# K_p transposed by DMA, batch 0's attention over both halves, and a divided last store in a fused Linformer attention and maxout kernel

## Chip, cores and metric

One core of a Trainium2 chip. The metric is the device time of one execution in microseconds; several executions are made and the median is given. Every kernel gave a correct result. Spans of profiles are some 1.8 us shorter than the device time of the same execution.

## The reference

```python
def _attn_ref(q, k, v, E, F):             # q, k, v: 8 x 8 x 1024 x 64
    k_proj = einsum('ks,bhsd->bhkd', E, k)      # K_p: 64 rows for 1024 tokens
    v_proj = einsum('ks,bhsd->bhkd', F, v)      # V_p
    attn = softmax(scale * q @ k_proj^T)
    return attn @ v_proj                        # x: 8192 x 512 after a transpose

def _moe_ref(x, w1, w2, w_out):           # 512 -> 1024 -> 512
    g = maximum(x @ w1, x @ w2)
    return g @ w_out                            # 8192 x 512, fp32
```

## The kernel before

Batches follow one another. While TensorE computes the output layer ("down") of one batch's units and the first layer ("up") of the next unit, the attention of the next batch is worked in between. The program is emitted slot by slot: a slot is one down product (12 matmuls, 1.31 us) and two up products (0.44 us each); 14 slots and one attention make a batch. "Slot -8" of a batch below means eight slots before its first one. The kernel uses max(a, b) = max(a - b, 0) + b: the up product is x(w1 - w2) (`wd`), and b's part goes through the product M = w2 w_out. From batch 1 on, the products are done with seven block products in place of eight.

These are the parts that the change and the argument touch. The copies out of the projection, and the transpose of K_p on TensorE through a PSUM bank:

```python
def step_kv(t, h0=0, h1=H, which="kv", att=False):
    kv_ps = att_banks()[:, 0, :] if att else mm_bank()
    ...                                              # the projection, 16 matmuls
    if "k" in which:
        eng(out=fl(t["kp"]), in_=kv_ps[0:KP, 0:n])               # ScalarE
    elif "v" in which: ...                                       # cut
        nc.vector.tensor_copy(out=fl(t["vp"][KP:128]), in_=kv_ps[KP:128, 0:n])
        nc.vector.tensor_copy(out=fl(t["vp"][0:KP]), in_=kv_ps[KP:128, 0:n])

def step_kpt(t, h0=0, h1=H, att=False):
    kpt_ps = att_banks(FP16)[:, 0, :] if att else mm_bank(FP16)
    for h in range(h0, h1):
        for r in range(2):
            nc.tensor.transpose(out=kpt_ps[...], in_=t["kp"][:, h, :], identity=ident16[:KP, :KP])
    nc.vector.tensor_copy(out=t["kpt"][...], in_=kpt_ps[...])
```

The loads of q, k and v, 2 MB each in DRAM and cast to fp16 on the way, are issued from GpSimd. Stores and the DMA transposes of q are issued from SyncE (SP in the profile), one after the other. The schedule for batches 3 to 7:

```python
at(b - 1, -11, 0, step_qt_dma, t, 0, H // 2)
at(b - 1, -11, 0, step_qt_dma, t, H // 2, H)
at(b - 1, -9, 0, step_kv, t, 0, H, "kv", True)
at(b - 1, -9, 0, loads, b + 1, "v", "q", "k")     # the next batch's v and q, and the k after it
at(b - 1, -8, 0, step_kpt, t, 0, H, True)
plan = "sc0 -7, da0 -6, sc1 -4, da1 -3, sc2 -1, da2 0, sc3 2, da3 3"   # sc0: the first scores; da0: their sums and the product with V_p
```

The softmax here doesn't subtract the row's maximum and nothing guards it: scores larger than these inputs give would overflow.

Of the kernel before, what the change touches and what calls it, by code (L numbers as in the profile page):

```python
# [16 lines left out]
def kernel(  # L17
# [82 lines left out]

    def load(t, n, src, b, h0, h1, c0=0, c1=NC):
        nc.gpsimd.dma_start(  # L102
            out=t[n][:, h0:h1, c0:c1, :],
            in_=src[b, h0:h1].rearrange("h (p c) d -> p h c d", c=NC)[:, :, c0:c1, :],
        )
# [4 lines left out]
    for h0 in (0, H // 2):  # L110
        load(tiles[0], "k", k, 0, h0, h0 + H // 2)
        load(tiles[0], "q", q, 0, h0, h0 + H // 2, 0, NC // 2)
        if h0 == 0:
            ident = const.tile([128, 128], FP32)
            make_identity(nc, ident)
# [6 lines left out]
    for f0 in range(0, DF, 256):  # L122
        if f0 == 256:
            load(tiles[0], "q", q, 0, 0, H, NC // 2, NC)
        for w_sb, w in ((w2_sb, moe_w2), (w1_sb, moe_w1)):
            nc.gpsimd.dma_start(
                out=w_sb[:, :, f0 : f0 + 256],
                in_=w[:, f0 : f0 + 256].rearrange("(r p) f -> p r f", p=128),
            )
# [34 lines left out]
    def new_attn(t):  # L164
        t["kp"] = proj.tile([KP, H, D], FP16, tag="kp", name="kp_sb")
        t["vp"] = proj.tile([128, H, D], FP16, tag="vp", name="vp_sb")
        t["kpt"] = proj.tile([128, H, KP], FP16, tag="kpt", name="kpt_sb")
        t["qt"] = qtp.tile([128, H, HALF], FP16, tag="qt", name="qt_sb")
        t["ex"] = {}


    def step_kv(t, h0=0, h1=H, which="kv", att=False):
# [14 lines left out]
        if "k" in which:  # L187
            eng = nc.vector.tensor_copy if which == "k" else nc.scalar.copy
            eng(out=fl(t["kp"]), in_=kv_ps[0:KP, 0:n])
        if both:  # L190
            nc.vector.tensor_copy(out=fl(t["vp"]), in_=kv_ps[:, 0:n])
        elif "v" in which:
            nc.vector.tensor_copy(out=fl(t["vp"][KP:128]), in_=kv_ps[KP:128, 0:n])
            nc.vector.tensor_copy(out=fl(t["vp"][0:KP]), in_=kv_ps[KP:128, 0:n])


    def step_kpt(t, h0=0, h1=H, att=False):
        kpt_ps = att_banks(FP16)[:, 0, :] if att else mm_bank(FP16)
        for h in range(h0, h1):
            for r in range(2):  # L200
                nc.tensor.transpose(
                    out=kpt_ps[r * D : (r + 1) * D, (h - h0) * KP : (h - h0 + 1) * KP],
                    in_=t["kp"][:, h, :],
                    identity=ident16[:KP, :KP],
                )
        nc.vector.tensor_copy(
            out=t["kpt"][:, h0:h1, :].rearrange("q h k -> q (h k)"),
            in_=kpt_ps[:, 0 : (h1 - h0) * KP],
        )

# [77 lines left out]
    def two_sc(t, g, j):  # L288
        sc_ps = att_banks()
        t["ps", g] = sc_ps  # L290
        for h in range(2):
            for o in range(2):
                for e in range(2):
# [7 lines left out]
                    )  # L301
        ex = stage.tile([128, 2, HALF], FP16, tag="ex", name="ex_sb")
        t["ex"][g] = ex
        nc.scalar.activation(out=ex, in_=sc_ps, func=ACTF.Exp, scale=scale)


    def two_dn(t, g):
        dn_ps = t.pop(("ps", g))
        for r in range(2):
            for e in range(2):  # L310
# [3 lines left out]
                    lhsT=ones16[rows, 0:D],  # L314
                    rhs=t["ex"][g][rows, e, :],
                    start=True, stop=True,
                )
        ld = soft.tile([128, 2, HALF], FP32, tag="ld", name="ld_sb")
        nc.scalar.activation(out=ld, in_=dn_ps, func=ACTF.Ln)
        nc.scalar.activation(out=ld, in_=ld, func=ACTF.Exp, scale=-1.0)  # L320
        rec = ld
        t["rec", g] = rec

    def two_at(t, g, j):
        ex, rec = t["ex"].pop(g), t.pop(("rec", g))
        at_ps = [mm_bank().rearrange("q (h n) -> q h n", h=2) for _ in range(2)]
# [26 lines left out]
    def up_slots(t, j):  # L353
        t["gt", j] = gt = gpool.tile([128, NFB, HALF], FP16, tag="gt", name="gt_sb")
        for fb in range(NFB):
            def up(fb=fb):
                h_ps = mm_bank()
                for r in range(NDC):
# [5 lines left out]
                    )  # L364
                nc.vector.tensor_scalar_max(gt[:, fb, :], h_ps, 0.0)
            yield up
# [237 lines left out]
    def down_steps(u, alone):  # L604
# [6 lines left out]

        def product(k, name, n):
            if n is not None:
# [13 lines left out]
            }[k]()  # L627
            for i in range(2):
                for c in range(NG + NX):
# [3 lines left out]
                        rhs=w_(c),  # L633
                        start=(n is not None and i == 0 and c == 0),
                        stop=(c == NG + NX - 1), skip_group_check=True,
# [12 lines left out]

        def store(j):
            nc.sync.dma_start(  # L650
                out=out.rearrange("(n p i o) m -> n o p i m", p=128, i=NI, o=2)[
                    b, o, :, 2 * j : 2 * j + 2, :
                ],
                in_=st["o", j],
            )
# [18 lines left out]
        def p3():  # L674
            add(0, 1, product(3, "Z", None), st["u1"])
            store(0)
            o_tile(1)
            add(1, 1, st["u2"], st["s5"])

        def p4():  # L680
            bank = product(4, "X", None)
            nc.scalar.copy(out=cols(st["o", 1], 0), in_=two(bank))
            store(1)
# [8 lines left out]
    warm(2)  # L692
    step_kpt(t, 0, 4)
    step_qt(t, 0, 4, 0, NI // 2)
    warm(2)
    two_sc(t, 0, 0)
    warm(2)
    step_kv(t, 4, 8, "k")
    two_dn(t, 0)
    step_qt(t, 4, 4, 0, NI // 2)  # L700
    step_kpt(t, 4, 8)
    warm(3)
    two_sc(t, 1, 0)
    warm(3)
    step_kv(t, 0, 4, "v")
    two_dn(t, 1)
    two_at(t, 0, 0)
    warm(3)
    step_kv(t, 4, 8, "v")
    step_w2t(0)  # L710
    step_wd(0)
    two_at(t, 1, 0)
    warm(6)

# [7 lines left out]
    def loads(b, *names):  # L722
# [5 lines left out]
    slots = [  # L728
        (0, u0[0]), (1, u0[1]), (None, f(step_qt, 0, 4, NI // 2, NI)),
        (None, f(step_qt, 4, 4, NI // 2, NI)), (None, lambda: loads(1, "v", "q", "k")),  # L730
        (None, lambda: warm(2)),
        (None, f(two_sc, 0, 1)), (None, f(two_sc, 1, 1)), (None, wd[1]), (2, u0[2]),
        (None, f(two_dn, 0)), (3, u0[3]), (None, f(two_dn, 1)), (None, wd[2]),
        (None, f(two_at, 0, 1)), (4, u0[4]), (5, u0[5]), (None, wt[1]), (None, wd[3]),
        (None, f(two_at, 1, 1)), (None, wt[2]), (6, u0[6]), (None, wt[3]), (7, u0[7]),
        *((8 + n, x) for n, x in enumerate(u1)),
        *((16 + n, lambda n=n: step_m(n)) for n in range(NDC)),
# [25 lines left out]
    for b in range(1, B):  # L763
# [26 lines left out]
        else:  # L790
            at(b - 1, -11, 0, new_attn, t)
            at(b - 1, -11, 0, step_qt_dma, t, 0, H // 2)
            at(b - 1, -11, 0, step_qt_dma, t, H // 2, H)
            at(b - 1, -9, 0, step_kv, t, 0, H, "kv", True)
            at(b - 1, -9, 0, loads, b + 1, "v", "q", "k")
            at(b - 1, -8, 0, step_kpt, t, 0, H, True)
            plan = "sc0 -7, da0 -6, sc1 -4, da1 -3, sc2 -1, da2 0, sc3 2, da3 3"
        for x in plan.split(", "):
            name, n = x.split()
# [64 lines left out]
```

## Time and profile before

| | before |
|---|---|
| device time, median | 347.74 us |
| span of the profile | 345.4 us |
| mean granted TensorE clock | 0.996 |
| TensorE (PE) busy | 332.9 us, 96% |
| period of one batch | 37.9 us |
| first matmul of the product M | 44.16 us |
| last matmul ends / last store lands | 340.45 / 344.10 us |

The page gives for each engine the time in which it was busy, and the chain of work that ended last, followed back from the end: whatever has a large share of that chain sets the time. Here TensorE has it, with no large wait. In the lines PE is TensorE, PEld its weight loads, DVE VectorE, ACT ScalarE, POOL GpSimd and SP SyncE, with a q behind the name for what stands in an engine's queue; L12 is line 12 of the kernel. The lines themselves stand in the prediction.

### The profile page before, as it was taken

The numbers are of one execution on the slowest core, as the hardware profiler recorded it, in microseconds if no ns is written. First come the engines' busy times: TensorE is split into PE (matmuls) and PEld (weight loads), VectorE is DVE, ScalarE is ACT, GpSimd is POOL, SyncE is SP. The second block draws the span as 40 slices with busy tenths as digits, with TensorE's granted clock in tenths as the row PEclk, the third lists the DMA queues.
The fourth block names the chain that finished last, engine by engine and source line by source line (L and its number), as shares of the span: only waits on it lengthen the run. The fifth ranks groups of instructions, "written<-read, shape, count | busy, mean of one in ns | idle before, by whom it ended". The sixth has DMA issues, their size and how long they took to land.

```text
span 345.4 us, 7094 instructions
## 1 busy us (share of the span) xinstructions
PE 332.9 (96%) x2979; PEld 233.5 (68%) x2979; DVE 232.4 (67%) x394; ACT 218.7 (63%) x325; POOL 31.5 (9%) x43
## 2 busy tenths in 40 slices
PE   8988999999999999999999999999999999999994
PEld 4543444434476777777777777777777777888883
DVE  1367717534787778686769778686869777777561
ACT  2437222773896778668884777668875788654541
POOL 8433002011103000120012000100000000000000
PEclk9999999999999999999999999999999999999998
DMA  8999999999998999799669949891923030303033
GB/s 154 200 197 201 207 207 193 238 159 260 174 205 183 195 208 250 109 191 193 173 114 181 222 122 172 150 200 20 199 47 123 2 121 2 121 5 123 0 123 121
DMA packets 65232, 52.36 MB, mean 152 GB/s; under 512 B 26160, under 2 KB 56880, under 8 KB 65200
## 3 DMA queue, kind: packets, MB, share of 16 engines
q0 software_dynamic: 31312, 28.31, 53.7%
q1 hardware_dynamic: 33888, 23.60, 25.2%
q8 instruction: 23, 0.38, 0.4%
q14 instruction: 9, 0.07, 0.1%
HBM read 57.15 MB, written 16.78 MB: 214 GB/s over the span
## 4 chain that ended last, share of the span: by engine, by line
PE 75%; DVE 9%; ACT 6%; DMA 6%; POOL 2%; issue 1%; DVEq 0%; ACTq 0%; POOLq 0%
PE mm_ps L630 31%; PE mm_ps L552 21%; PE mm_ps L385 5%; DMA big<-in_moe_w_dram 4%; PE mm_ps L359 4%; PE att_ps L265 4%; PE att_ps L180 3%; DVE big L496 2%; PE att_ps L241 2%; DVE xt_sb L279 2%; ACT ld_sb L272 2%; DVE gt_sb L567 2%; PE mm_ps L425 2%; ACT ld_sb L275 2%; PE mm_ps L520 2%
## 5 line engine op out<-in xcount | busy, mean ns | idle before, releaser
L506 ACT COPY p_sb<-mm_ps 128x512 f32<-128x512 f32 x160 | 89.1, 592 | 44.0 <-PE mm_ps L630 29.6
L630 PEld LDWEIGHTS <-big 128*128 128x128 f16 x672 | 65.7, 98 | 8.1 <-DVE big L496 0.5
L630 PE MATMUL mm_ps<-T_sb,big 128*128 128x256 f16 x504 | 61.6, 273 | 0.3 <-DVE big L496 0.3
L279 DVE TENSOR_TENSOR xt_sb<-att_ps,ld_sb 128x1024 f16<-128x1024 f32 x28 | 34.2, 1221 | 29.2 <-ACT ld_sb L275 29.1
L567 DVE TENSOR_TENSOR gt_sb<-mm_ps,p_sb 128x512 f16<-128x512 f32 x52 | 35.8, 689 | 22.4 <-PE mm_ps L552 22.4
L552 PEld LDWEIGHTS <-big 128*128 128x128 f16 x416 | 38.9, 98 | 12.7 <-issue 8.5
L552 PE MATMUL mm_ps<-big 128*128 128x256 f16 x312 | 43.7, 273 | 0.3 <-DVE gt_sb L567 0.3
L552 PEld LDWEIGHTS <-wd_sb 128*128 128x128 f16 x312 | 28.2, 98 | 13.8 <-issue 10.7
L630 PEld LDWEIGHTS <-gt_sb 128*128 128x128 f16 x336 | 32.7, 98 | 4.2 <-DVE gt_sb L570 0.2
L630 PE MATMUL mm_ps<-wo_sb,gt_sb 128*128 128x256 f16 x224 | 33.7, 273 | 0.0
L552 PE MATMUL mm_ps<-xt_sb,wd_sb 128*128 128x256 f16 x208 | 31.0, 273 | 2.3 <-DVE gt_sb L567 2.3
L249 ACT ACTIVATE ex_sb<-att_ps 128x1024 f16<-128x1024 f32 x28 | 28.9, 1031 | 4.2 <-PE att_ps L241 4.2
L272 ACT ACTIVATE ld_sb<-att_ps 128x1024 f32<-128x1024 f32 x28 | 28.9, 1030 | 3.5 <-PE att_ps L265 3.5
L275 ACT ACTIVATE ld_sb<-ld_sb 128x1024 f32<-128x1024 f32 x28 | 30.0, 1070 | 0.4
L646 DVE TENSOR_TENSOR o_sb<-mm_ps,p_sb 128x512 f32<-128x512 f32 x28 | 19.3, 689 | 12.1 <-PE mm_ps L630 12.1
L630 PE MATMUL mm_ps<-m_sb,xt_sb 128*128 128x256 f16 x112 | 21.4, 273 | 0.0
L102 POOL DMA_DIRECT2D v_sb<-in_v_dram x9 | 7.7, 863 | 145.1 <-DMA qt_sb<-q_sb 120.8
L570 DVE TENSOR_SCALAR gt_sb<-gt_sb 128x512 f16<-128x512 f16 (+1 forms) x52 | 19.1, 367 | 1.8
L496 DVE TENSOR_TENSOR big<-gt_sb 128x1024 f16<-128x1024 f16 x28 | 19.2, 685 | 0.9
L602 ACT ACTIVATE gt_sb<-mm_ps 128x512 f16<-128x512 f32 x26 | 15.6, 599 | 4.7 <-PE mm_ps L552 4.7
L630 PEld LDWEIGHTS <-xt_sb 128*128 128x128 f16 x168 | 16.4, 98 | 1.9
L567 DVE TENSOR_TENSOR gt_sb<-p_sb 128x512 f16<-128x512 f32 x26 | 17.7, 681 | 0.0
(94 smaller groups left out, 455.4 us busy)
## 6 DMA issues: line engine op xcount, KB each, us to landing
out_dram<-o_sb SPq DMA_DIRECT2D x28, 512.0 KB, 3.1
k_sb<-in_k_dram POOLq DMA_DIRECT2D x7, 1024.0 KB, 18.2
v_sb<-in_v_dram POOLq DMA_DIRECT2D x7, 1024.0 KB, 9.9
q_sb<-in_q_dram POOLq DMA_DIRECT2D x7, 1024.0 KB, 13.6
big<-in_moe_w_dram POOLq DMA_DIRECT2D x8, 256.0 KB, 14.3
out_dram<-o_sb SPq DMA_DIRECT2D x8, 256.0 KB, 4.6
k_sb<-in_k_dram POOLq DMA_DIRECT2D x2, 512.0 KB, 7.8
v_sb<-in_v_dram POOLq DMA_DIRECT2D x2, 512.0 KB, 12.5
```

The lines of the kernel that those rows point to most:

```text
L249: nc.scalar.activation(out=ex, in_=sc_ps, func=ACTF.Exp, scale=scale)
L272: nc.scalar.activation(out=ld, in_=dn_ps, func=ACTF.Ln)
L275: nc.scalar.activation(out=ld, in_=ld, func=ACTF.Exp, scale=-1.0)
L279: nc.vector.tensor_tensor(out=t["xt"][:, p, :, :], in0=at_ps, in1=ld, op=ALU.mult)
L385: nc.tensor.matmul(out=op_ps, lhsT=lhsT, rhs=rhs, start=(n == 0), stop=(n == NFB + NDC - 1),)
L496: nc.vector.tensor_tensor(out=S(i), in0=x, in1=y, op=op)
L506: nc.scalar.copy(out=x, in_=bank)
L552: nc.tensor.matmul(out=bank[:, m * W : (m + 1) * W], lhsT=w_[:, n_, (2 * d + m) * 128 : (2 * d + m + 1) * 128], rhs=a[:, n_, :], start=(n ...
L567: nc.vector.tensor_tensor(out=c_blk(j, c), in0=two(x), in1=two(y), op=ALU.add)
L570: nc.vector.tensor_scalar_max(ap, ap, 0.0)
L630: nc.tensor.matmul(out=bank[:, i * CH : (i + 1) * CH], lhsT=a(c)[:, i * 128 : (i + 1) * 128], rhs=w_(c), start=(n is not None and i == 0 a ...
L646: nc.vector.tensor_tensor(out=cols(st["o", j], c), in0=two(x), in1=two(y), op=ALU.add)
```

## The change

It has three independent parts. At the start, batch 0's q is loaded whole ahead of the weights, its attention runs over both halves of the blocks, and the up slots alternate between the halves. In the middle, K_p of batches 3 to 7 is transposed by a DMA and not by TensorE; for this the K_p tile holds each head twice, and the copies of V_p are deferred by one slot (this in batches 1 and 2 as well). At the end, the last output tile is stored in three parts.

```diff
-        load(tiles[0], "q", q, 0, h0, h0 + H // 2, 0, NC // 2)
+        load(tiles[0], "q", q, 0, h0, h0 + H // 2)
...
-        t["kp"] = proj.tile([KP, H, D], FP16, tag="kp", name="kp_sb")
+        t["kp"] = proj.tile([KP, H, 2, D], FP16, tag="kp", name="kp_sb")
...
         elif "v" in which:
-            nc.vector.tensor_copy(out=fl(t["vp"][KP:128]), in_=kv_ps[KP:128, 0:n])
-            nc.vector.tensor_copy(out=fl(t["vp"][0:KP]), in_=kv_ps[KP:128, 0:n])
+            def finish_v():
+                nc.vector.tensor_copy(out=fl(t["vp"][KP:128]), in_=kv_ps[KP:128, 0:n])
+                if att:
+                    nc.vector.tensor_copy(out=kp[:, :, 1, :], in_=kp[:, :, 0, :])
+                    step_kpt_dma(t)
+                nc.vector.tensor_copy(out=fl(t["vp"][0:KP]), in_=fl(t["vp"][KP:128]))
+
+            return finish_v
...
+    def step_kpt_dma(t):
+        nc.sync.dma_start_transpose(
+            out=t["kpt"], in_=t["kp"].rearrange("p h r d -> p (h r d)")
+        )
...                                  # start: attention over both halves, alternating up slots
+                if fb < 3:
+                    nc.scalar.activation(out=gt[:, fb, :], in_=h_ps, func=ACTF.Relu)
+                else:
+                    nc.vector.tensor_scalar_max(gt[:, fb, :], h_ps, 0.0)
...                                  # end: the last tile in three stores
+            if alone:
+                store(1, m0=CH)
...
-            at(b - 1, -11, 0, new_attn, t)
-            at(b - 1, -11, 0, step_qt_dma, t, 0, H // 2)
-            at(b - 1, -11, 0, step_qt_dma, t, H // 2, H)
-            at(b - 1, -9, 0, step_kv, t, 0, H, "kv", True)
-            at(b - 1, -9, 0, loads, b + 1, "v", "q", "k")
-            at(b - 1, -8, 0, step_kpt, t, 0, H, True)
+            at(b - 1, -12, 0, new_attn, t)
+            at(b - 1, -12, 0, step_qt_dma, t, 0, H // 2)
+            at(b - 1, -12, 0, step_qt_dma, t, H // 2, H)
+            at(b - 1, -9 if b == 3 else -10, 2 if b == 3 else 0, step_kv, t, 0, H, "kv", True)
+            at(b - 1, -7, 0, loads, b + 1, "v", "q", "k")
             plan = "sc0 -7, da0 -6, sc1 -4, da1 -3, sc2 -1, da2 0, sc3 2, da3 3"
+            if b == 3:
+                plan = "sc0 -5, da0 -4, sc1 -3, da1 -2, sc2 -1, da2 0, sc3 2, da3 3"
```

More of the change, by code (lines that the diff above doesn't have):

```diff
@@ L99, in load_all, with load @@
         load(t, n, src, b, 0, H)
-    def load(t, n, src, b, h0, h1, c0=0, c1=NC):
+    def load(t, n, src, b, h0, h1):
         nc.gpsimd.dma_start(
-            out=t[n][:, h0:h1, c0:c1, :],
-            in_=src[b, h0:h1].rearrange("h (p c) d -> p h c d", c=NC)[:, :, c0:c1, :],
+            out=t[n][:, h0:h1],
+            in_=src[b, h0:h1].rearrange("h (p c) d -> p h c d", c=NC),
         )
@@ L122 @@
     for f0 in range(0, DF, 256):
-        if f0 == 256:
-            load(tiles[0], "q", q, 0, 0, H, NC // 2, NC)
         for w_sb, w in ((w2_sb, moe_w2), (w1_sb, moe_w1)):
@@ L188, in step_kv @@
             eng = nc.vector.tensor_copy if which == "k" else nc.scalar.copy
-            eng(out=fl(t["kp"]), in_=kv_ps[0:KP, 0:n])
+            kp = t["kp"][:, h0:h1]
+            eng(out=kp[:, :, 0, :], in_=kv_ps[0:KP, 0:n].rearrange("p (h d) -> p h d", d=D))
         if both:
@@ L192, in step_kv, with step_kpt @@
         elif "v" in which:
-            nc.vector.tensor_copy(out=fl(t["vp"][KP:128]), in_=kv_ps[KP:128, 0:n])
-            nc.vector.tensor_copy(out=fl(t["vp"][0:KP]), in_=kv_ps[KP:128, 0:n])
-    def step_kpt(t, h0=0, h1=H, att=False):
-        kpt_ps = att_banks(FP16)[:, 0, :] if att else mm_bank(FP16)
+            def finish_v():
[5 more added lines that the diff above has]
+            return finish_v
+    def step_kpt(t, h0=0, h1=H):
+        kpt_ps = mm_bank(FP16)
         for h in range(h0, h1):
@@ L202, in step_kpt @@
                     out=kpt_ps[r * D : (r + 1) * D, (h - h0) * KP : (h - h0 + 1) * KP],
-                    in_=t["kp"][:, h, :],
+                    in_=t["kp"][:, h, 0, :],
                     identity=ident16[:KP, :KP],
@@ L289, in two_sc @@
         sc_ps = att_banks()
-        t["ps", g] = sc_ps
+        t["ps", g, j] = sc_ps
         for h in range(2):
@@ L301, in two_sc, with two_dn @@
                     )
-        ex = stage.tile([128, 2, HALF], FP16, tag="ex", name="ex_sb")
-        t["ex"][g] = ex
-        nc.scalar.activation(out=ex, in_=sc_ps, func=ACTF.Exp, scale=scale)
-    def two_dn(t, g):
-        dn_ps = t.pop(("ps", g))
+        pool, tag = (ppool, "pu") if (g, j) == (1, 1) else (stage, "ex")
+        t["ex", g, j] = pool.tile([128, 2, HALF], FP16, tag=tag, name="ex_sb")
+        nc.scalar.activation(out=t["ex", g, j], in_=sc_ps, func=ACTF.Exp, scale=scale)
+    def two_dn(t, g, j):
+        dn_ps = t.pop(("ps", g, j))
         for r in range(2):
@@ L314, in two_dn, with two_inv @@
                     lhsT=ones16[rows, 0:D],
-                    rhs=t["ex"][g][rows, e, :],
+                    rhs=t["ex", g, j][rows, e, :],
                     start=True, stop=True,
                 )
-        ld = soft.tile([128, 2, HALF], FP32, tag="ld", name="ld_sb")
-        nc.scalar.activation(out=ld, in_=dn_ps, func=ACTF.Ln)
-        nc.scalar.activation(out=ld, in_=ld, func=ACTF.Exp, scale=-1.0)
-        rec = ld
-        t["rec", g] = rec
+        pool, tag = (soft, "ld") if g == 0 else (opool, "o")
+        t["rec", g, j] = pool.tile([128, 2, HALF], FP32, tag=tag, name="ld_sb")
+        nc.scalar.activation(out=t["rec", g, j], in_=dn_ps, func=ACTF.Ln)
+    def two_inv(t, g, j):
+        rec = t["rec", g, j]
+        nc.scalar.activation(out=rec, in_=rec, func=ACTF.Exp, scale=-1.0)
     def two_at(t, g, j):
-        ex, rec = t["ex"].pop(g), t.pop(("rec", g))
+        ex, rec = t.pop(("ex", g, j)), t.pop(("rec", g, j))
         at_ps = [mm_bank().rearrange("q (h n) -> q h n", h=2) for _ in range(2)]
@@ L364, in up @@
                     )
-                nc.vector.tensor_scalar_max(gt[:, fb, :], h_ps, 0.0)
+                if fb < 3:
+                    nc.scalar.activation(out=gt[:, fb, :], in_=h_ps, func=ACTF.Relu)
+                else:
+                    nc.vector.tensor_scalar_max(gt[:, fb, :], h_ps, 0.0)
             yield up
@@ L610, in cat, with product @@
             return lambda n: g[:, n] if n < NG else x[:, n - NG]
-        def product(k, name, n):
+        def product(k, name, n, part=(0, 1)):
             if n is not None:
@@ L627, in product @@
             }[k]()
-            for i in range(2):
+            for i in part:
                 for c in range(NG + NX):
@@ L633, in product @@
                         rhs=w_(c),
-                        start=(n is not None and i == 0 and c == 0),
+                        start=(n is not None and i == part[0] and c == 0),
                         stop=(c == NG + NX - 1), skip_group_check=True,
@@ L647, in add, with store @@
                 out=cols(st["o", j], c), in0=two(x), in1=two(y), op=ALU.add)
-        def store(j):
+        def store(j, i0=0, i1=2, m0=0, m1=DM):
             nc.sync.dma_start(
                 out=out.rearrange("(n p i o) m -> n o p i m", p=128, i=NI, o=2)[
-                    b, o, :, 2 * j : 2 * j + 2, :
+                    b, o, :, 2 * j + i0 : 2 * j + i1, m0:m1
                 ],
-                in_=st["o", j],
+                in_=st["o", j][:, i0:i1, m0:m1],
             )
@@ L678, in p3 @@
             add(1, 1, st["u2"], st["s5"])
+            if alone:
+                store(1, m0=CH)
         def p4():
+            if alone:
+                for i in range(2):
+                    bank = product(4, ("C", i), 2 + i, (i,))
+                    part = slice(i * CH, (i + 1) * CH)
+                    nc.vector.tensor_tensor(
+                        out=st["o", 1][:, i, 0:CH], in0=bank[:, part], in1=st["u2"][:, part],
+                        op=ALU.add,
+                    )
+                    store(1, i, i + 1, 0, CH)
+                return
             bank = product(4, "X", None)
@@ L693 @@
     step_kpt(t, 0, 4)
+    warm(2)
     step_qt(t, 0, 4, 0, NI // 2)
+    step_qt(t, 0, 4, NI // 2, NI)
     warm(2)
     two_sc(t, 0, 0)
+    two_sc(t, 0, 1)
     warm(2)
     step_kv(t, 4, 8, "k")
-    two_dn(t, 0)
+    two_dn(t, 0, 0)
+    warm(2)
+    step_kpt(t, 4, 8)
+    two_dn(t, 0, 1)
+    two_inv(t, 0, 0)
+    warm(4)
     step_qt(t, 4, 4, 0, NI // 2)
-    step_kpt(t, 4, 8)
-    warm(3)
+    step_qt(t, 4, 4, NI // 2, NI)
+    warm(2)
     two_sc(t, 1, 0)
-    warm(3)
+    two_sc(t, 1, 1)
     step_kv(t, 0, 4, "v")
-    two_dn(t, 1)
+    two_dn(t, 1, 0)
+    two_inv(t, 1, 0)
     two_at(t, 0, 0)
-    warm(3)
+    two_dn(t, 1, 1)
+    two_inv(t, 0, 1)
     step_kv(t, 4, 8, "v")
-    step_w2t(0)
+    two_inv(t, 1, 1)
     step_wd(0)
     two_at(t, 1, 0)
-    warm(6)
+    two_at(t, 0, 1)
+    warm(4)
     load_all(tiles[1], 1, "k", k)
@@ L728 @@
     slots = [
-        (0, u0[0]), (1, u0[1]), (None, f(step_qt, 0, 4, NI // 2, NI)),
-        (None, f(step_qt, 4, 4, NI // 2, NI)), (None, lambda: loads(1, "v", "q", "k")),
-        (None, lambda: warm(2)),
-        (None, f(two_sc, 0, 1)), (None, f(two_sc, 1, 1)), (None, wd[1]), (2, u0[2]),
-        (None, f(two_dn, 0)), (3, u0[3]), (None, f(two_dn, 1)), (None, wd[2]),
-        (None, f(two_at, 0, 1)), (4, u0[4]), (5, u0[5]), (None, wt[1]), (None, wd[3]),
-        (None, f(two_at, 1, 1)), (None, wt[2]), (6, u0[6]), (None, wt[3]), (7, u0[7]),
-        *((8 + n, x) for n, x in enumerate(u1)),
+        (0, u0[0]), (None, f(two_at, 1, 1)), (1, u0[1]), (None, lambda: loads(1, "v", "q", "k")),
+        (None, wd[1]), (2, u1[0]), (3, u1[1]), (4, u0[2]), (None, wt[0]), (5, u0[3]),
+        (None, wd[2]), (None, wt[1]), (6, u1[2]), (7, u1[3]), (8, u0[4]), (9, u0[5]), (None, wd[3]),
+        (None, wt[2]), (10, u1[4]), (11, u1[5]), (12, u0[6]), (13, u0[7]), (None, wt[3]),
+        (14, u1[6]), (15, u1[7]),
         *((16 + n, lambda n=n: step_m(n)) for n in range(NDC)),
```

## The prediction

> **What bounds the kernel now.** I read the page first (busy time, chain), then the busy time by stretch, then the timeline and the chain where the change touches. In the page, busy times of the engines and the chain that ended last:
>
> ```profile
> PE 332.9 (96%) x2979; PEld 233.5 (68%) x2979; DVE 232.4 (67%) x394; ACT 218.7 (63%) x325; POOL 31.5 (9%) x43
> ...
> PE 75%; DVE 9%; ACT 6%; DMA 6%; POOL 2%; issue 1%; DVEq 0%; ACTq 0%; POOLq 0%
> ```
>
> TensorE is the bound: 75% of the chain, and hardly idle. So only three things can save: less PE work in the middle, less PE waiting at the start, a shorter tail. The stretches of one batch period (columns: span, then PE, PEld, DVE, ACT, POOL busy, clock, DMA share, GB/s) show how regular the middle is:
>
> ```profile
> 144.80:182.80 38.00, 37.54 (x363) 28.86 (x364) 28.80 (x50) 27.90 (x43) 2.63 (x3) 1.00 0.89 170
> 182.80:220.70 37.90, 37.44 (x362) 28.80 (x364) 28.67 (x50) 27.91 (x43) 2.72 (x3) 1.00 0.86 162
> ```
>
> 37.9 us a batch, of which PE waits about 0.5 (a wait for a DVE add at 160.5, once a batch). The start, in the timeline (start, us, engine, line, what, count, idle before):
>
> ```profile
> 21.82 0.69 DVE L403 TENSOR_TENSOR wd_sb<-big,big 128x1024 f16<-128x1024 f16 x1 [0.68 <-DMA big<-in_moe_w_dram]
> ...
> 36.39 7.93 PE L359 MATMUL mm_ps<-xt_sb,wd_sb 128*128 128x512 f16 x36
> ...
> 44.16 7.07 PE L425 MATMUL mm_ps<-wo_sb,big 128*128 128x512 f16 x32
> ```
>
> From 22.6 to 36.4 the up products come singly, between the second half's attention and waits for weight chunks; from 36.4 PE is dense. An up slot is four matmuls, and 36 take 7.77 us on the chain, so 0.86 us a slot. Where a gain at the start ends up is told by the chain around 80 us:
>
> ```profile
> 76.88 0.92 ACT ld_sb L272
> 77.79 4.48 DMA out_dram<-o_sb
> ...
> 82.35 0.59 ACT o_sb L392
> 82.94 0.48 ACT kp_sb L189
> ...
> 83.44 0.69 DVE vp_sb L193
> ...
> 84.15 0.70 DVE vp_sb L194
> ...
> 84.89 1.89 PE mm_ps L520 x8
> ```
>
> An output copy (L392) waits for an output buffer, whose store stands on SP behind this transfer, which itself waits for batch 2's q to land:
>
> ```profile
> 71.24 6.50 SPq L229 DMA_TRANSPOSE qt_sb<-q_sb  x1
> ```
>
> That landing is set by one uninterrupted stream of loads from the first microsecond, and the change leaves its bytes as they are. So 82.35 is a fixed point.
>
> [...] each change to 64-row tiles and back leaves a hole of 0.10 us in the starts. [...] A 64x512 PSUM copy is 0.69 here; I estimate 0.3 for the SBUF one (the fp16 in-place max at L570, 128x512, is 0.29). [...] a 512 KB store beside loads (first row, 140 to 165 us) against one with no loads left (second row, 240 to 265; columns count, size, us to landing):
>
> ```profile
> out_dram<-o_sb SPq DMA_DIRECT2D x2, 512.0 KB, 7.3
> ```
> ```profile
> out_dram<-o_sb SPq DMA_DIRECT2D x4, 512.0 KB, 2.8
> ```
>
> **The change part by part.**
>
> Start. Batch 0's q whole (512 KB more) goes ahead of the first weights. The stream lands a 512 KB piece in about 2.7 us (second k half at 12.15 with a 256 KB q piece at 13.45 after it), so the first weight pair lands at 24.4 instead of 21.73; later chunks land as before, since the later q load is gone. The built order puts the first wd subtraction on DVE before six of the multiplies that finish batch 0's attention, so: wd 24.5 to 25.2, multiplies (0.65 each) to 27.7, the last two after their own matmuls, 28.1 to 29.4. The first up is at 26.7, the fifteen others from 28.1: 15 x 0.86 = 12.9, and four w2 transposes of about 0.5 = 2.0, so the M product starts at 43.1 instead of 44.16. Gain 1.1 (0 to 1.5); three ups of each half now leave by ACT, which was idle there.
>
> Up to 85 us this meets the fixed point. The second vp copy now reads SBUF, so the bank of L180 is free after one PSUM copy, at 84.2, and L520 starts there instead of at 84.89. Of the 1.1, 0.7 survives; the rest becomes PE waiting at 84.
>
> Middle, batches 3 to 7. The 16 PE transposes of K_p disappear:
>
> ```profile
> 148.59 0.38 PE L630 MATMUL mm_ps<-T_sb,xt_sb 128*128 128x256 f16 x2
> ...
> 148.90 0.44 PE L201 MATMUL att_ps<-ident,kp_sb 64*64 64x64 f16 x16
> ...
> 149.27 0.61 PE L552 MATMUL mm_ps<-big,wd_sb 128*128 128x256 f16 x4
> ```
>
> The two matmuls before take 2 x 0.109 = 0.22, to 148.81; the next stream starts at 149.27. So 0.46 a batch, 5 x 0.46 = 2.3. DVE loses a 0.42 copy and gains a short one; it is not the bound. In exchange kpt comes by a DMA transpose (128 KB). Batch 3's scores start two slots later, which may remove one 0.5 wait (121.9 us): 0.3.
>
> End. The last product is stored in two 128 KB pieces, and the other half of the tile goes early. Before, the last matmul ends at 340.47, ACT copies until 341.08, the store lands at 344.1, the span ends at 345.4. Now DVE does both short adds (about 0.37 each) after two adds of 0.69 that end at 340.54, so to 341.3: later by 0.2, but with a fourth of the bytes in the last store. Net gain 0.4.
>
> Sum: 0.7 + 2.3 + 0.3 + 0.4 = 3.7, so 344.0 with nothing lost.
>
> **The rivals.** First, the K_p DMA takes the place of the transposes as a wait. In the built order the projection of batches 4 to 7 ends at slot 4 and the scores come at slot 7; between them PE has two up products (0.44 each), two whole slots (1.31 + 2 x 0.44 = 2.18 each), a down product (1.31) and one more up: 0.87 + 4.36 + 1.31 + 0.44 = 7.0 us. In that time: ACT copy 0.6, vp copy 0.7, duplicate 0.3 with queueing about 2.2, then the DMA. For it the profile is bad: q and k loads are released by the same projection, and the store issued at 149.62, after them, took 9.9 us to land (the longest of L650), 4 of them before its first byte. 128 KB in 256-byte packets beside loads took some 3.6 us in the transpose at 71.24. An estimate from these: 7 us, arrival 9.2 us after the projection, a PE wait of 2.2 for batches 4 to 6 (7 has no loads beside it), and for batch 3, with a store in front, up to 5: 11.6 in all, and 355.6. Against it: the change moves the projection and q transposes a slot earlier and batch 3's scores two slots later, which looks like a writer who saw this wait and tuned it away, and left batches 4 to 7 at slot 7 because they needed no more. I weigh these as half no wait, three tenths some 3 us, two tenths the full cost.
>
> Second, the gain at the start is hidden altogether by the fixed point, or the first weights come late enough to make it negative (if M starts after 44.5, PE loses what it is late): 0.7 less to 0.5 worse, 344.7 to 345.5.
>
> Third, the start gains more because the fixed point moves forward[...]: then the full 1.1 + 0.3 survive and it is 343.3.
>
> **Range and chances.** 344.0 without the K_p wait, 347 with some of it, 355.6 with all. The middle of that mixture is 345.5; 341.8 allows for a start 1 us better and no wait of PE's own at 160, 352.5 for two thirds of the K_p wait. Faster by over 2% is below 340.8, which needs twice the gain that I can count: 0.05. Slower by over 2% is above 354.7, the full K_p wait: 0.10. Within: 0.85.
>
> **What would show it.** M's first matmul (L441 there) at 43 rather than 44.2; the third plain up product of batch 1 (now L536) near 84.2 with PE idle before it; batch periods of 37.4 instead of 37.9; no idle time of PE at the score matmuls (L252) of batches 3 to 6, released by the DMA into kpt. If those rows show waits of 2 us or more, the first rival holds; if the third up product is earlier than 83.5, my fixed point was none, and the prediction is too slow.

## The result, and the profile after

The changed kernel takes 374.19 us in the median (373.78 to 374.93, 4 runs) beside 347.49 for the kernel before in the same rounds: ratio 1.0766, 95% interval 1.0737 to 1.0796. It is slower by 7.7%, where the prediction had a time 0.6% below that of before.

The page of the changed kernel, busy times, granted clock in 40 slices of the span, and the chain that ended last:

```profile
PE 339.5 (91%) x2896; PEld 236.5 (63%) x2896; DVE 226.9 (61%) x390; ACT 222.2 (60%) x330; POOL 30.6 (8%) x42
...
PEclk9999999999999699979999699996999999999998
...
PE 73%; DMA 13%; DVE 8%; ACT 4%; issue 1%; DVEq 0%; POOLq 0%
```

TensorE has fewer instructions than before, yet it is busy for longer; four times, some 40 us apart, the clock digit falls to 6 or 7. And DMA now has 13% of the chain. The group of the scores, on the same page (busy time, mean ns, then idle time of the engine just before and what ended it):

```profile
L252 PE MATMUL att_ps<-qt_sb,kpt_sb 64*64 64x512 f16 x112 | 12.4, 433 | 20.7 <-DMA kpt_sb<-kp_sb 20.7
```

TensorE stood idle for 20.7 us before score matmuls, all of it until the DMA into `kpt_sb`. The chain shows one of these waits, that of batch 4 (start, us, what):

```profile
154.15 0.42 PE mm_ps L568 x4
154.57 9.98 DMA kpt_sb<-kp_sb
164.54 0.04 issue
164.59 0.64 PE att_ps L252 x4
```

The transpose was issued at 154.57 and landed 9.98 us later. All five, by the source line that issues them, landed after:

```profile
L218 SPq DMA_TRANSPOSE kpt_sb<-kp_sb x5: 1196/1510/1979, 111.9 to 288.9; - x5
...
DMA to landing us min/median/max: 2.7/9.3/12.1
```

In order they took 12.1 us for batch 3, then 10.0, 9.3 and 8.5, and 2.7 for batch 7, which has no loads beside it. Batch 7 is the only one without a wait at its scores. The same two stretches that the prediction shows for before (span, then PE, PEld, DVE, ACT, POOL busy with counts, clock, DMA share, GB/s):

```profile
144.80:182.80 38.00, 31.97 (x278) 23.75 (x276) 22.27 (x40) 22.10 (x35) 2.66 (x3) 0.91 0.75 128
182.80:220.70 37.90, 32.45 (x282) 24.17 (x282) 23.92 (x41) 22.90 (x36) 2.69 (x3) 0.91 0.92 161
```

TensorE started 278 matmuls in 38 us where it had started 363, and the clock is 0.91. Each of the four waits ran into one stretch of 6.83 us at half clock; the second of the four:

```profile
162.90:169.73 6.83, 5.14 (x28) 3.19 (x32) 1.92 (x4) 1.11 (x2) 0.00 (x0) 0.50 1.17 263
```

In the four stretches TensorE was busy for 4.75, 5.14, 4.66 and 5.10 us, 19.65 in all, and at half clock it did what takes half of that: in the second one the 128x256 matmuls started 0.21 us apart (165.99 to 166.84), against 0.11 at full clock (112.12 to 112.56). My estimate of the loss is therefore 19.65 / 2 = 9.8 us. The waits and the clock together are 20.7 + 9.8 = 30.5 us.

The start, in the timeline:

```profile
25.29 0.68 DVE L419 TENSOR_TENSOR wd_sb<-big,big 128x1024 f16<-128x1024 f16 x1
...
43.84 2.54 PE L441 MATMUL mm_ps<-wo_sb,big 128*128 128x512 f16 x11
```

The first subtraction starts at 25.29 (24.5 was predicted) and M at 43.84 (43.1 was predicted, 44.16 before). And the place that the prediction called a fixed point:

```profile
71.42 5.98 SPq L240 DMA_TRANSPOSE qt_sb<-q_sb  x1
...
81.69 0.59 ACT L408 COPY o_sb<-mm_ps 128x512 f32<-128x512 f32 x1 [2.42 <-DMA out_dram<-o_sb]
...
84.61 1.90 PE L536 MATMUL mm_ps<-xt_sb,wd_sb 128*128 128x512 f16 x8 [0.28 <-DVE vp_sb L193]
```

The output copy still waits for its store, but it starts at 81.69, not at 82.35. The third up product starts at 84.61, 0.28 ahead of the kernel before, and it waits for the deferred V_p copy.

### The profile page after: what moved, and what is told of

Same layout as the page of the kernel before. It is cut to its first block, busy times and chain, and to the rows that moved or that the text cites. A ratio compares the mean times of both kernels' runs of the same rounds, so it can differ in the third digit from the quotient of the medians.

```text
span 373.0 us, 6933 instructions
## 1 busy us (share of the span) xinstructions
PE 339.5 (91%) x2896; PEld 236.5 (63%) x2896; DVE 226.9 (61%) x390; ACT 222.2 (60%) x330; POOL 30.6 (8%) x42
## 4 chain that ended last, share of the span: by engine, by line
PE 73%; DMA 13%; DVE 8%; ACT 4%; issue 1%; DVEq 0%; POOLq 0%
PE mm_ps L646 28%; PE mm_ps L568 19%; DMA kpt_sb<-kp_sb 11%; PE mm_ps L401 6%; PE att_ps L276 4%; PE mm_ps L372 3%; PE att_ps L252 3%; DMA k_sb<-in_k_dram 2%; PE mm_ps L178 2%; PE att_ps L178 2%; DVE xt_sb L290 2%; PE mm_ps L441 2%; PE mm_ps L536 2%; DVE big L512 2%; ACT ld_sb L283 1%; ACT ld_sb L286 1%
## 5 line engine op out<-in xcount | busy, mean ns | idle before, releaser
L646 PEld LDWEIGHTS <-big 128*128 128x128 f16 x672 | 66.3, 99 | 8.8 <-DVE big L512 0.5
L646 PE MATMUL mm_ps<-T_sb,big 128*128 128x256 f16 x504 | 62.9, 276 | 0.3 <-DVE big L512 0.3
L568 PEld LDWEIGHTS <-big 128*128 128x128 f16 x416 | 40.1, 100 | 11.8 <-issue 6.6
L568 PE MATMUL mm_ps<-big 128*128 128x256 f16 x312 | 45.1, 278 | 0.5 <-DVE gt_sb L583 0.5
L646 PEld LDWEIGHTS <-gt_sb 128*128 128x128 f16 x336 | 33.9, 102 | 5.8 <-issue 0.6
L646 PE MATMUL mm_ps<-wo_sb,gt_sb 128*128 128x256 f16 x224 | 36.5, 289 | 0.0
L568 PE MATMUL mm_ps<-xt_sb,wd_sb 128*128 128x256 f16 x208 | 32.2, 281 | 1.7 <-DVE gt_sb L583 1.7
L252 PE MATMUL att_ps<-qt_sb,kpt_sb 64*64 64x512 f16 x112 | 12.4, 433 | 20.7 <-DMA kpt_sb<-kp_sb 20.7
L646 PE MATMUL mm_ps<-m_sb,xt_sb 128*128 128x256 f16 x112 | 22.9, 288 | 0.0
L252 PEld LDWEIGHTS <-kpt_sb 64*64 64x64 f16 x112 | 3.2, 106 | 28.2 <-DMA kpt_sb<-kp_sb 21.9
```

The source lines that it names most:

```text
L252: nc.tensor.matmul(out=sc_ps[pos : pos + KP, e, :], lhsT=t["kpt"][o * D : (o + 1) * D, 2 * p + e, :], rhs=t["qt"][o * D : (o + 1) * D, 2 * ...
L568: nc.tensor.matmul(out=bank[:, m * W : (m + 1) * W], lhsT=w_[:, n_, (2 * d + m) * 128 : (2 * d + m + 1) * 128], rhs=a[:, n_, :], start=(n ...
L646: nc.tensor.matmul(out=bank[:, i * CH : (i + 1) * CH], lhsT=a(c)[:, i * 128 : (i + 1) * 128], rhs=w_(c), start=(n is not None and i == par ...
```

## The experiments

**Theory.** The whole loss comes from K_p's DMA transpose: it takes about four times as long as alone (8.5 to 12.1 us against 2.7) because the next batch's loads are issued just before it, so TensorE waits, and each wait (4.2 to 5.9 us) brings the 6.83 us at half clock that it ran into. **Rivals.** The new start or the deferred copies cost as well; the transpose is slow by itself, or because of SP's stores; the halved clock is only a mark beside the wait.

**1. K_p on TensorE again (kpt_pe).**

```diff
-                if att:
-                    nc.vector.tensor_copy(out=kp[:, :, 1, :], in_=kp[:, :, 0, :])
-                    step_kpt_dma(t)
...                                  # and, for batches 3 to 7, the schedule of before
+            at(b - 1, -8, 0, step_kpt, t, 0, H, True)
```

> The changed kernel with one thing undone: for batches 3 to 7 K_p is transposed on TensorE again, with the slots of the kernel before for these batches; the start, the deferred V_p copies and the split last store stay. My theory (the DMA transpose of K_p is the whole loss, through waits of 21.4 us at the first scores of batches 3 to 6 and through the halved clock that follows each): no wait there, full clock from 20 us to the end, 343.5 to 346 us, a ratio of 0.99 to 0.997 to the kernel before. Rival (the new start or the deferred copies cost too, hidden under the waits): above 348.

347.31 us (346.58 to 347.88) beside 347.11; ratio 0.999, interval 0.9956 to 1.0024. The waits and the four stretches at half clock are gone, and the stretch of one batch is that of the kernel before:

```profile
182.40:220.30 37.90, 37.45 (x362) 28.77 (x364) 28.75 (x50) 27.91 (x43) 2.62 (x3) 1.00 0.87 166
```

So the loss is all in the K_p part. But the median came out above my range, which says that the start and the tail together give nearly nothing. Experiments 8 to 10 take that up.

**2. The K_p part alone (kpt_only).** The kernel before, with the diff's lines for the K_p tile, the deferred copies, the DMA and the schedule, and with the old start and the old tail.

> The kernel before with the K_p part alone: DMA transpose of K_p for batches 3 to 7, the doubled K_p tile, the deferred copies and the shifted slots; old start, old tail. My theory: nearly all of the loss is here: waits of 4 to 6 us at the first scores of batches 3 to 6, four stretches of 6.8 us at half clock, 372 to 377 us. Rival (the loads of the new start push the loads of the later batches onto the transposes, so that it needs both parts): waits under 3 us and under 362 us.

376.88 us (374.9 to 378.68), ratio 1.0841, interval 1.0782 to 1.09. The row of the scores on its page:

```profile
L254 PE MATMUL att_ps<-qt_sb,kpt_sb 64*64 64x512 f16 x112 | 12.4, 433 | 23.8 <-DMA kpt_sb<-kp_sb 23.8
```

The wait is there without the new start. Both of the first two runs agree: this part is the loss.

**3. Dummy work in the wait (warm).**

```diff
     def step_sc(t, p):
         sc_ps = att_banks()
+        if p == 0 and t.get("dma"):               # batches 3 to 6
+            for _ in range(20):
+                nc.tensor.matmul(
+                    out=sc_ps[:, 0, :], lhsT=ones16[:, 0:128], rhs=ones16, start=True, stop=True
+                )
```

> The changed kernel with 20 dummy matmuls (about 4.3 us) into the score bank just before the first scores of batches 3 to 6, so that TensorE works while K_p is on its way. They separate the wait from the halved clock. My theory: the scores still start when the K_p transpose has landed (9 to 12 us after its issue), but the granted clock stays at full in the middle, and some 9 us of the 27 go: 363 to 367 us. Rival (the clock record is only a mark beside the wait and TensorE does not lose by it): 372 to 376.

368.59 us (365.75 to 369.95), ratio 1.0593, interval 1.0537 to 1.0649: 5.6 us below the changed kernel and above my range. The row of the scores, and the stretch that was at half clock:

```profile
L258 PE MATMUL att_ps<-qt_sb,kpt_sb 64*64 64x512 f16 x112 | 11.5, 400 | 6.5 <-DMA kpt_sb<-kp_sb 6.5
```
```profile
162.90:170.00 7.10, 6.44 (x60) 4.69 (x59) 2.93 (x6) 4.32 (x7) 0.00 (x0) 1.00 1.12 261
```

The clock is full. TensorE idles for 6.5 us and does 80 dummies of 0.216 us, 17.3: the scores wait 23.8 us in all, 3.1 more than the 20.7 of the changed kernel, since K_p happened to land later in this run; and M started 0.8 later. The changed kernel's span of 373.0 + 3.1 + 0.8 - 9.8 gives 367.1; the span was 367.5. The estimate of 9.8 us for the clock holds, and the rival that took it for a mere mark is out.

**4. The loads held until K_p has landed (hold).**

```diff
                     step_kpt_dma(t)
+                    nc.gpsimd.tensor_copy(out=held, in_=t["kpt"][0:1, 0, 0:8])
```

The three loads stand behind this copy of eight values in GpSimd's program. In batch 4 of this run the transpose was issued at 145.72 and landed 2.7 us later, the copy ran at 148.57, and the first load was issued at 149.11.

> The changed kernel with one tiny GpSimd copy out of the transposed K_p ahead of the three loads of the next batch, so that these loads are issued only when K_p has landed. My theory (the K_p transpose takes 8.5 to 12 us only because three 2 MB loads were issued just before it; beside none it took 2.7): K_p lands 2.5 to 4 us after its issue, the waits at the first scores of batches 3 to 6 are gone or below 1 us, the clock is full, 342 to 347 us. Rival one (the time is the transpose's own, or SP's stores): it still lands 8 us or more after issue, 370 or more. Rival two (the loads, held by 5 to 9 us, come too late for the next projection or its q transposes): new waits there, 350 to 365.

344.03 us (343.55 to 345.21), ratio 0.9902, interval 0.9871 to 0.9933: 30 us less than the changed kernel for one tiny instruction a batch. The chain, by engine; the transposes' times from issue to landing; and the timeline of batch 4:

```profile
PE 84%; DVE 7%; ACT 4%; DMA 2%; issue 1%; DVEq 0%; POOLq 0%
```
```profile
DMA to landing us min/median/max: 2.7/2.7/3.2
```
```profile
145.72 1.20 SPq L220 DMA_TRANSPOSE kpt_sb<-kp_sb  x1
...
149.11 0.88 POOL L102 DMA_DIRECT2D v_sb<-in_v_dram  x1 [0.36 <-issue]
...
150.04 0.41 PE L254 MATMUL att_ps<-qt_sb,kpt_sb 64*64 64x512 f16 x4
```

K_p lands in 2.7 to 3.2 us, and no wait is left at the scores. The loads, issued after the transpose's landing and not before its issue, are still in time everywhere. Both rivals of this run fall: the time is not the transpose's own and not the stores' (in batch 3 a store still moves on SP's queue ahead of the transpose, and it landed in 3.2), and the held loads bring no new wait.

**5. The loads beside the transpose and not before it (hold_kp).** As hold, but the tiny copy reads the doubled K_p tile, the transpose's source: in batches 4 to 6 the loads are issued about 0.6 us after the transpose. In batch 3, where SP is still busy with a store, the first load goes out 0.25 us before it.

> As the run that held the loads until the transposed K_p had landed, but the tiny GpSimd copy reads the doubled K_p tile that the transpose reads, so that the three loads are issued at about the same time as the transpose, not after its landing and not before its issue. It tells two rivals apart. If what matters is that the load packets stand ahead of the transpose's packets when it is issued: K_p lands within 3 to 5 us, waits at the first scores below 1.5 us, 343 to 348 us. If what matters is that the packets share the engines while they run: K_p still takes 7 us or more, waits of 3 us or more and half clock after them, 358 us or more.

353.5 us (352.34 to 355.84), ratio 1.0165, interval 1.0147 to 1.0184: between the two. In the profiled run the transposes of batches 4, 6 and 7 landed in about 2.8 us and those of batches 3 and 5 in about 10 and 9, with waits of 3.8 and 4.6 us. Batch 3's had the store and the first load ahead of it; batch 5's was issued first, like those of batches 4 and 6, and shows why that may not be enough. The DMA queues in two stretches, 190.0 to 191.5 and 191.5 to 195.0 (packets, MB, share of the 16 engines):

```profile
q1 hardware_dynamic: 512, 0.13, 61.3%
q0 software_dynamic: 6, 0.01, 8.1%
```
```profile
q0 software_dynamic: 384, 0.39, 104.4%
```

q1 is the queue of SP, q0 that of GpSimd's loads. All 512 packets of the transpose had moved by 191.5. Then the load began, and for 3.9 us, from 191.4 to 195.3, q1 moved nothing at all, not even the transpose's 32 small packets (4 bytes each in the changed kernel, where batches 4 and 5 landed 0.29 and 0.32 us after the last of them); it landed at 197.75. The same silence stands at the beginning of the transpose in the changed kernel, from its issue at 154.6 to 158.0:

```profile
q0 software_dynamic: 531, 0.54, 108.5%
```

There is no row of q1. The transpose's first packet moved 3.96 us after its issue here, and 4.43 and 4.01 us after in batches 5 and 6; with no loads (batch 7, and batches 4 to 7 of hold) it took 1.17. After that the two queues share; the stretch from 161.0 to 162.5:

```profile
q0 software_dynamic: 224, 0.22, 93.6%
q1 hardware_dynamic: 222, 0.06, 33.4%
```

One packet of the transpose moves for one of the loads, but the former has 256 bytes and the latter 1 KB. So batch 4's 512 data packets took 5.5 us, where they took 1.05 in hold. Of the 7.3 us that this transpose lost, about 2.8 lie in the silence and about 4.5 in the sharing.

Neither of my two rivals was right as I had put them: being issued first helped in this run where the data and the small packets were both through when the loads began. In batches 4 and 6 of hold_kp the last of the small packets went 0.06 and 0.03 us before the first packet of the loads; in batch 5 only the data was through, by 0.03 us. These packets show the loads moving alone (for 3.9 us in hold_kp; in the changed kernel from each transpose's issue to its first packet, 3.96 to 4.43 us), and then both queues. The length is not fixed: in batches 4 and 6 of hold_kp SP's next packets, a store's, moved 1.1 and 1.5 us after the loads' first. Why the loads move alone for so long was not settled.

**6. Batch 3's slots for all (hold_plan).** On top of hold:

```diff
-            if b == 3:
+            if b >= 3:
                 plan = "sc0 -5, da0 -4, sc1 -3, da1 -2, sc2 -1, da2 0, sc3 2, da3 3"
```

> The kernel with the held loads, and batch 3's attention slots (first scores two slots later, all four pairs nearer together) for batches 3 to 7. In the held run the 0.64 us wait after the second scores was gone for batch 3, which has these slots, and stood in batches 4 to 7. If it hangs on the slots: no such wait, 4 x 0.64 = 2.6 us less than the held run (342.3 us of span), 341 to 342 us in the median. Rival (batch 3 lacks it for another reason, or the later scores bring new waits at the sums for the next unit): 344 or more.

343.42 us (341.93 to 344.2, 6 runs), ratio 0.9883, interval 0.9865 to 0.9901. That is above my range, although the wait is gone as expected. The matmuls after the second scores, in hold and then in this run:

```profile
158.56 0.60 PE L570 MATMUL mm_ps<-xt_sb,wd_sb 128*128 128x256 f16 x4 [0.46 <-DVE gt_sb L585]
```
```profile
156.01 0.61 PE L570 MATMUL mm_ps<-big,wd_sb 128*128 128x256 f16 x4
```

In hold the projections of batches 4 to 7 come 37.47 us apart, here 37.38, 37.02 and 37.02. So a batch gains 0.45, which is what the profile calls the wait for VectorE (0.46). The 0.64 of my expectation was the whole hole in TensorE's work; the other 0.2 us are there with these slots as well. In this profile the scores of batch 2 came 0.9 us later than in hold, so that in this execution half of the gain of 1.8 us (four times 0.45) is gone; the medians differ by 0.6. The spread of the start is taken up below.

**7. Two issuers for the last stores (best).** As hold_plan, with the very last store issued by ScalarE.

> As the run before it, and the last of the split stores of the tail is issued by ScalarE instead of SyncE. In the traces with the split tail SyncE took 0.76 and 0.60 us to issue the last two stores one behind the other, and the last store landed 3.87 to 3.92 us after TensorE's end, against 3.65 with the tail of before. With two issuers I expect 3.3 to 3.5, so 0.4 us less than the run before it: below 341.5. Rival (the landing is bound by the transfers and not by the issue): no difference.

342.42 us (341.68 to 343.17), ratio 0.9857, interval 0.9841 to 0.9873, which overlaps that of hold_plan. In the trace nothing was gained: the last store landed 3.89 us after TensorE's last matmul, as with the divided stores of the other runs (3.87 to 3.92). The expectation was wrong. SP's last store, now with no other behind it, was issued at 336.75 and landed at 340.06, later than ScalarE's (339.82). Side by side the two stores took 3.31 and 2.87 us to land, where one behind the other they took 2.91 and 2.46 in hold_plan: the time from issue to landing bounds the end here, not the queue of issues.

**8. The start alone (start_only).** The kernel before with the start's lines of the diff.

> The kernel before with the start alone: batch 0's q whole ahead of the weights, its attention over both halves, up slots alternating, three of eight relus of each half on ScalarE. My prediction gave it 1.1 us at the M product and 0.7 at the end. The traces of the other runs show the M product at 43.5 to 44.6 with this start and at 43.9 to 44.2 with the old one. I expect -0.5 to +0.3 us, a ratio of 0.998 to 1.001, so nothing that can be told from noise. If the predicted gain is real: 0.997 or lower.

345.96 us (345.46 to 347.15, 6 runs) beside 347.32; ratio 0.9963, interval 0.9948 to 0.9978. My expectation for this run, nothing, was wrong: the predicted gain is real, and larger at the end than the 0.7 us that the prediction let survive. A line of its timeline:

```profile
80.69 0.58 ACT L395 COPY o_sb<-mm_ps 128x512 f32<-128x512 f32 x1 [2.01 <-DMA out_dram<-o_sb]
```

The output copy of the fixed point starts at 80.69 here, 1.7 earlier than before, and M started at 43.26. Nothing makes TensorE wait at 84 us. The place of M in one profile is weak evidence, though: with the old start it lies at 43.88, 44.16 and 46.00 in three runs, with the new one between 42.77 and 44.63.

**9. The start with the deferred V_p copies (start_defer).** As start_only, with both V_p copies after the next slot and the second one out of SBUF, but no DMA.

> The kernel before with the new start and the deferral of the V_p copies (both copies after the next slot, the second one out of SBUF), without K_p's DMA and without the new tail. The start alone was -1.36 us (0.9963). If the deferral makes TensorE wait 0.45 us for VectorE at the third plain up product of batch 1: that wait is in the trace, and the ratio is 0.997 to 0.9985. Rival (the difference between the start alone and the changed kernel's start is spread between executions): no such wait and 0.9963 again.

346.55 us (345.51 to 347.45), ratio 0.997, interval 0.9948 to 0.9992. The ratios do not tell the two runs apart; the trace shows the wait that I had expected:

```profile
84.82 1.46 PE L526 MATMUL mm_ps<-xt_sb,wd_sb 128*128 128x512 f16 x6 [0.28 <-DVE vp_sb L192]
```

By the starts of its matmuls TensorE is idle for 0.44 us here, as in the changed kernel (0.45) and nearly as in the kernel before (0.41), where start_only has a hole of 0.10 (the 0.28 in the line counts from the modelled ends): the deferred copy comes behind a 0.69 us max on VectorE and frees the projection's bank that much later. The six executions also show where the spread comes from. The three with a mean clock of 0.991 to 0.993 took 347.05 to 347.45 us, the three with 0.994 or more 345.51 to 346.05. The changed kernel's profile, too, has 3.41 us at half clock from 9.30 on; so have those of start_defer and tail_only near the same place (mean clocks of these two profiles 0.993 and 0.991), while those of the kernel before, start_only and best2 (0.996, 0.997 and 0.998) have none before 100 us. Whether such a stretch falls into the start differs from execution to execution; in these six the two groups are 1.4 us apart.

**10. The tail alone (tail_only).** The kernel before with the divided last store.

> The kernel before with the split last store alone. My prediction gave it -0.4 us. The traces of the other runs, in which the last store landed 3.87 to 3.92 us after TensorE's end with the split store and 3.65 with the undivided one, say +0.25. Expected a ratio of 1.000 to 1.001; if the prediction's -0.4 is right, 0.999. The profile decides, by the time from the last matmul's end to the last landing.

348.09 us (347.56 to 349.01) beside 347.52; ratio 1.0017, interval 0.9998 to 1.0036. In its trace the last matmul ends at 342.17 and the last store lands at 346.07: 3.90 us, against 340.45 to 344.10, 3.65, before. By the traces the tail costs 0.25 us; the ratio alone can't tell it from nothing.

**11. What helped, together (best2).** hold_plan, with the undivided last store and with V_p undeferred in batches 1 and 2.

```diff
-            return finish_v
+            if att:
+                return finish_v
+            finish_v()
...
-            if alone:
+            if False:                      # the divided stores of the last tile
```

> The kernel with held loads and batch 3's slots for all, with the undivided last store of the kernel before, and with the V_p copies of batches 1 and 2 undeferred. Each should give a little: the undivided store landed 3.65 us after TensorE's end against 3.9 for the split one (0.25), and the start alone, without the deferral, had no wait before the third plain up product where the runs with the deferral have 0.45. Expected 0.7 less than the run with held loads and batch 3's slots, whose ratio was 0.9883: ratio 0.985 to 0.987, 341.7 to 342.8 us. Rival (both are noise): 0.988 or more.

342.17 us (341.04 to 342.59, 5 runs) beside 347.52; ratio 0.9843, interval 0.9821 to 0.9865. It beats both kernels: 1.6% under the kernel before and 32 us under the changed one. The two last steps alone can't be told from hold_plan and best by the ratios; the profile has the third up product without a wait and the last store 3.64 us after the last matmul. Its page:

```profile
PE 329.2 (97%) x2896; PEld 231.5 (68%) x2896; DVE 224.6 (66%) x388; ACT 221.1 (65%) x331; POOL 32.9 (10%) x47
...
PE 86%; DMA 5%; DVE 4%; POOL 2%; issue 1%; ACT 1%; DVEq 0%; POOLq 0%
```

## Why the prediction was wrong, and where it was right

**The bound.** TensorE bounds the kernel; right, before and in best2 alike.

**0.46 us a batch from the dropped transposes.** Right. The matmul after the second scores recurs after 37.94 us in the kernel before (160.52, 198.46) and after 37.47 in hold (158.56, 196.03): 0.47.

**Batch 3's plan removes one wait.** Right; and it would have done so for the other batches too, once K_p was on time.

**The start.** The 1.1 us at M is of the right size: 0.9 in the profile of start_only, and 1.36 in the medians. The fixed point at 82.35 was none: in start_only the same copy starts at 80.69. The third rival had said that it might move, but not why it did. The step that failed is "one uninterrupted stream of loads from the first microsecond". In the kernel before, GpSimd was idle for 23.6 us before it issued batch 2's v and q at 53.37, released by TensorE's projection of batch 1; in start_only it issued them at 52.47, earlier by the same 0.90 us as M, and q landed at 70.38 in place of 71.15. The k load ahead of them, the last of the stream, landed at 58.05 and 58.04, so loading batch 0's q whole did not speed it up. The step "the bank of L180 is free after one PSUM copy, at 84.2" failed: deferred, that copy queues behind VectorE's max, the bank came free at about 84.55 in the changed kernel, and TensorE waits 0.45 us. (The copy out of SBUF itself took 0.29, as estimated.)

**The tail.** The predicted gain of 0.4 was a loss of 0.25. The step that failed is "with a fourth of the bytes in the last store": two 128 KB stores landed 2.5 to 3.0 us after issue, much like the one of 256 KB (3.0), and SP took some 0.75 and 0.60 us to issue the two halves, against 0.37 for the whole one.

**"344.0 with nothing lost".** hold is the changed kernel with just the wait taken away, and its median is 344.03. That it meets the 344.0 is partly luck: the errors of the sum cancel in part (more from the start, less from the tail), and in its own rounds the gain was 3.1 us (from 347.11), where the sum had 3.7.

**The K_p wait.** The prediction named the mechanism, as the first rival, and got its size and its chance wrong. The term "7 us from issue to landing" was 10.0, 9.3 and 8.5 in batches 4 to 6, and 12.1 in batch 3. The wait was 20.7 us where the rival had 11.6. In batch 4 the transpose was issued 2.7 us after the projection's end (2.2 in the prediction) and TensorE had 7.1 us of other work (7.0): 2.7 + 10.0 - 7.1 = 5.6, the wait that the profile has. So the mis-sized term is the transfer. The profile of before had shown a store beside these loads that took 9.9 us to land; I took a smaller number than the one measured for the same situation. The chance was wrong by a worse step: "looks like a writer who saw this wait and tuned it away". The profile was set aside for a guess about the intention behind the code. The odds did not fit one another either: the full wait, 355.6, had two tenths, but everything above 354.7 only one. Two smaller slips: two thirds of 11.6 on 344.0 make 351.7, not 352.5, and a start 0.5 us worse than no gain makes 345.2, not 345.5.

**The clock.** No step of the prediction has it. In the traces each of the changed kernel's four waits, 4.2 to 5.9 us long, ran into 6.83 us at a granted clock of 0.50, and hold_kp, with waits of 3.8 and 4.6 us, had a mean clock of 0.981 where hold, without such waits, had 0.995. In the 3.41 us, half a stretch, ahead of the first and the second stretch (118.53 to 121.94 and 159.49 to 162.90) no matmul started; in those ahead of the third and the last, 203.87 to 207.28 and 248.24 to 251.65, TensorE was busy for 0.58 and 0.94 us. How long a wait must be, and how much work it may hold, to bring the half clock was not shown. So a wait that I put at 2 to 5 us had a second price, 9.8 us in all, a third of what was lost. The sum closes: hold's span of 342.3 plus 20.7 plus 9.8 is 372.8, and the changed kernel's span was 373.0.

**What stays open.** Why the loads keep SP's queue silent for some 3 to 4 us before the two share. The two silences hold 531 and 384 load packets, 33 and 24 for each of the 16 engines; no run here shows what begins or ends them.

## What to carry to other kernels

A small DMA on the critical path should not be issued into bulk loads: this one took three to over four times as long there as alone (8.5 to 12.1 us against 2.7). Just ahead of them it is a gamble (in hold_kp one of three was caught, and took about 9 us where the others took 2.8). The cure is to let the loads wait for it, which here cost nothing because they had slack (in hold it landed in 2.7 to 3.2 us and the loads brought no new wait). When a change may put a wait of several microseconds on TensorE, add the halved clock to its price (here 9.8 us on 20.7 us of waits). And where the profile has already measured a transfer of the same kind in the same place, use that number, whatever the code seems to intend.
